# A seven-product form for the first channel product of the last three batches and the tail

## The chip, the cores and the metric

The kernel runs on one core of a Trainium2 chip. The metric is the device time in microseconds of one execution, the median over runs. A profiled execution gives a span, from the first to the last instruction, which is a few microseconds shorter than the device time.

## The reference

Two stages. The first is a linear attention with random features: q and k are projected onto 128 features, put through an exponential, and the output is `q_p @ (k_p.T @ v)` over `q_p @ sum(k_p)`. Its result, per batch 576 tokens by 512, goes into an MLP mixer:

```python
xt = x.transpose(0, 2, 1)
h  = np.maximum(xt @ w_tok1, 0.0) @ w_tok2      # token product, 576 -> 256 -> 576
u  = x + h.transpose(0, 2, 1)
h2 = np.maximum(u @ w_ch1, 0.0) @ w_ch2         # channel product, 512 -> 1536 -> 512
return u + h2
```

There are 8 batches. The change concerns `u @ w_ch1`, the first channel product, and the relu behind it.

## The kernel before

Tokens 0 to 511 of a batch are worked as one block of 512 columns; the 64 last tokens of all eight batches are put together into a ninth block, called the tail (c = 8 in the code, `c == B`). All matmul operands are f16, PSUM sums are f32.

**Order.** Nothing is scheduled by the compiler. Each step is a job with an engine, made by `add`; the jobs are numbered as they are made, and the list `ORDER` at the head of the file gives the order in which they are issued, for all engines at once. So each engine has a fixed queue, and works it in order. `SLOT` gives the ring slot (PSUM bank, SBUF buffer) that each job takes, and `MOVED` the jobs that run on another engine than usual. The stages of neighbouring batches are interleaved: while TensorE does the channel products of batch c, it also does the attention of batch c+1 and the token product.

**A batch on the engines.** Attention (`attention`): TensorE projects (jobs `kp`, `qp`, `kt`, `qt`), ScalarE takes the exponential out of PSUM, VectorE takes a maximum per key (`km`: a reduction over 1,024 elements and a reciprocal; one for each pair of heads, four in a batch), GpSimd scales v with it (`vs_`), TensorE sums over keys (`kv`), and its result, copied to SBUF, is multiplied with q (`num`); VectorE divides (`num_out`). Token product (`token_mix`): `t1_tail`, `t1`, relu, `t2`, then VectorE adds x (`uadd`, four in a batch) and a DMA on SyncE's queue transposes u into uT. Every second batch adds the tails of two batches (`token_tail`).

**First channel product** (`channel_mix`, L967): for each of the 12 blocks of 128 channels, four matmuls of 512 columns over the four blocks of d go into one bank, and one relu (ScalarE, or VectorE where the lists say so) writes r3 in f16. That is 48 matmuls of 512 columns, each with a weight load, for each of the batches and the tail.

**Second channel product** (`channel_out_fast`, L917, L906): from batch 1 on it is done with seven half-size products in place of eight (Strassen's method in Winograd's form). VectorE makes four sums of r3 for each of two parts of 768 elements (the job `go` with g and k, the helper `tt` at L295). Each product is 12 matmuls of 256 columns; the partial results are summed in three banks X, Y and Z, and VectorE reads a bank after each step (`read`, L906). Four sums of the weights are made once (L448).

**Rings.** qT, kT and v (the loaded inputs), x and r1 have three slots each; there are eight PSUM banks.

Of the kernel before, what the change touches and what calls it, by code (L numbers as in the profile page):

```python
# [9 lines left out]
FP32 = mybir.dt.float32  # L10
# [12 lines left out]
    4, 3, 0, 2, 5, 7, 1, 6, 16, 14, 10, 15, 9, 8, 12, 38, 11, -1, -2, -3, -4, -5, -6, -7, -8, 39, 41, 13, 44,  # L23
    42, 21, 40, 47, 45, 48, 76, 22, 46, 77, 67, 43, 68, -4, -6, 120, 18, 105, 78, 107, 82, -3, 49, 71, 106, 122,
    -5, 90, 51, 111, 91, -4, -4, 52, 17, 70, 19, 121, 50, 53, 83, 54, 92, 126, -5, -5, -5, -1, -1, -6, -3, -1,
    72, 69, 30, 108, 79, 110, 84, 112, 80, 96, 55, 81, 127, 113, 74, 73, 123, 109, 75, 28, 128, 124, 85, 114,
    86, 57, 56, 97, 115, 88, 129, 87, 125, -8, 61, 20, 93, 89, 98, 94, 23, 116, 130, 134, 95, 131, 31, 99, 117,
    132, 135, 219, 118, 103, 133, 119, 136, 104, 62, 100, 146, 101, 63, 220, 142, 221, 137, 58, 196, 143, 64,
    102, 24, 59, 144, 25, 147, 60, 66, 138, 460, 145, 205, 139, 65, 197, 222, 225, 140, 223, 206, 29, 148, 199,
    141, 224, 33, 247, 198, 149, 207, 233, 326, 250, 200, 235, 160, 251, 249, 211, 208, 32, 162, 234, 248, 201,  # L30
    156, 210, 253, 161, 158, 157, 163, 330, 174, 209, 254, 202, 236, 170, 238, 226, 237, 172, 204, 27, 159, 227,
    26, 166, 252, 325, 203, 255, 212, 171, 150, 256, 173, 239, 153, 167, 331, 257, 213, 151, 214, 154, 240, 258,
    259, 164, 155, 260, 152, 327, 217, 228, 215, 175, 241, 165, 332, 168, 242, 243, 245, 229, 244, 231, 181,
    169, 176, 246, 216, 182, 232, 177, 230, 218, 183, 261, 186, 262, 329, 264, 263, 328, 178, 265, 184, 266,
    179, 34, 272, 268, 273, 187, 269, 270, 267, 188, 271, 275, 274, 189, 333, 383, 276, 334, 355, 191, 335, 356,
    385, 180, 192, 336, 384, 185, 357, 369, 389, 386, 337, 370, 372, 193, 388, 459, 373, 35, 277, 374, 390, 194,
    36, 293, 371, 461, 387, 278, 465, 358, 294, 341, 361, 338, 295, 359, 360, 285, 343, 375, 362, 340, 344, 342,
    291, 464, 346, 286, 339, 376, 391, 37, 363, 462, 297, 364, 345, 296, 365, 377, 366, 289, 298, 392, 347, 378,
    367, 463, 393, 290, 381, 281, 368, 395, 348, 379, 282, 287, 394, 466, 380, 349, 195, 283, 396, 350, 597,
    382, 351, 353, 595, 284, 299, 354, 292, 190, 352, 279, 288, 300, 478, 397, 280, 472, 400, 473, 305, 306,  # L40
    398, 401, 301, 480, 302, 309, 479, 399, 474, 307, 492, 310, 503, 494, 489, 408, 303, 505, 402, 493, 409,
    406, 504, 403, 313, 490, 407, 491, 404, 314, 467, 506, 308, 517, 316, 304, 519, 405, 468, 469, 518, 410,
    315, 317, 508, 509, 520, 475, 311, 476, 598, 318, 510, 521, 470, 507, 321, 596, 523, 319, 471, 419, 320,
    524, 495, 413, 420, 600, 522, 511, 477, 525, 312, 433, 496, 512, 599, 526, 411, 434, 601, 481, 421, 412,
    414, 513, 323, 527, 497, 528, 425, 482, 498, 514, 529, 429, 729, 426, 602, 501, 530, 515, 431, 516, 734,
    499, 483, 735, 500, 417, 731, 322, 415, 730, 484, 502, 485, 423, 416, 432, 430, 486, 487, 422, 427, 488,
    418, 628, 424, 428, 608, 531, 610, 532, 435, 609, 436, 534, 439, 630, 440, 533, 443, 441, 535, 442, 629,
    437, 538, 444, 542, 642, 539, 653, 540, 438, 654, 536, 644, 541, 447, 324, 543, 655, 537, 643, 625, 448,
    656, 544, 639, 658, 545, 659, 640, 450, 626, 627, 546, 733, 641, 445, 657, 451, 611, 645, 614, 603, 455,
    605, 732, 616, 604, 631, 612, 646, 449, 615, 613, 606, 555, 632, 551, 607, 556, 617, 563, 647, 564, 633,  # L50
    552, 559, 648, 618, 456, 557, 560, 634, 1004, 446, 547, 867, 660, 567, 548, 866, 635, 661, 568, 649, 565,
    662, 558, 452, 665, 458, 736, 651, 561, 666, 652, 865, 553, 650, 619, 562, 637, 549, 620, 554, 638, 621,
    636, 623, 550, 663, 569, 664, 453, 624, 570, 622, 745, 571, 773, 746, 667, 572, 670, 566, 573, 747, 575,
    668, 775, 576, 774, 454, 579, 669, 577, 457, 671, 578, 869, 737, 748, 574, 739, 759, 672, 750, 580, 749,
    676, 673, 678, 738, 761, 677, 674, 760, 583, 740, 675, 585, 679, 584, 680, 787, 765, 762, 776, 586, 778,
    763, 764, 868, 766, 581, 587, 777, 788, 779, 741, 789, 790, 873, 591, 871, 875, 791, 588, 1001, 792, 582,
    1006, 767, 874, 742, 751, 923, 743, 695, 780, 589, 592, 696, 870, 925, 752, 924, 685, 590, 594, 999, 744,
    876, 693, 872, 753, 768, 694, 793, 781, 1000, 689, 686, 754, 782, 771, 699, 772, 794, 757, 755, 769, 758,
# [1013 lines left out]
```

## Time and profile before

| | |
|---|---|
| device time, median of 3 runs | 284.88 us |
| the runs | 284.88, 283.5, 285.11 us |
| span of the profiled execution | 281.1 us |
| TensorE busy | 270.3 us (96%) |
| VectorE busy | 222.4 us (79%) |
| ScalarE busy | 138.6 us (49%) |
| GpSimd busy | 92.0 us (33%) |

The device time of the profiled execution itself is not listed; the three runs lie 2.4 to 4.0 us above its span. In the profile PE is TensorE's matmul queue, PEld its weight loads, DVE VectorE, ACT ScalarE, POOL GpSimd and SP SyncE. A row of a group gives busy time and mean duration; on all engines an instruction's duration overlaps a little with the next one's start, so what an instruction takes of its queue is read from the starts of two neighbours in the timeline.

### The profile page before, as it was taken

Reading aid. Unit: us, or ns where it says so; the run is one execution under the profiler, and the core shown is the slowest. Engines: PE = TensorE matmul, PEld = TensorE weight load, DVE = VectorE, ACT = ScalarE, POOL = GpSimd, SP = SyncE. Lnnn points to the kernel's source line nnn. Section 1 sums busy time; section 2 is a strip of 40 time slices with the busy share of each in tenths; the row PEclk is TensorE's granted clock in tenths of the full one; section 3 lists DMA queues with packets and bytes.
Section 4 is the critical chain, followed back from the end, with each engine's and each line's share of the span. In section 5 each row is a group of like instructions: output and inputs, shape, how many; then the busy total and the mean of one; then the engine's idle time right before and its main releaser. Section 6 shows DMA issues by size and latency. Waiting matters only on the chain.

```text
span 281.1 us, 6278 instructions
## 1 busy us (share of the span) xinstructions
PE 270.3 (96%) x2526; PEld 167.6 (60%) x2526; DVE 222.4 (79%) x462; ACT 138.6 (49%) x288; POOL 92.0 (33%) x116
## 2 busy tenths in 40 slices
PE   6899999999999999999999999999999999999993
PEld 2547546443657755665667647755676467446782
DVE  2589828499999899996997999977995893565992
ACT  1498994049676418743758445734753510031200
POOL 8574994007510872048008710510033000000001
PEclk9999999999999999999999999999999999999999
DMA  6999999999998999997979993960151304030125
GB/s 161 194 189 161 157 169 213 178 191 202 179 218 184 148 172 186 181 198 104 212 178 185 241 135 101 161 156 2 76 97 59 111 0 96 0 149 2 75 90 135
DMA packets 80524, 39.66 MB, mean 141 GB/s; under 512 B 63984, under 2 KB 76016, under 8 KB 80304
## 3 DMA queue, kind: packets, MB, share of 16 engines
q0 software_dynamic: 31744, 17.74, 44.1%
q1 hardware_dynamic: 46832, 15.77, 29.1%
q10 hardware_dynamic: 1920, 5.77, 5.4%
q8 instruction: 19, 0.31, 0.4%
q14 instruction: 9, 0.07, 0.1%
HBM read 35.95 MB, written 16.52 MB: 187 GB/s over the span
## 4 chain that ended last, share of the span: by engine, by line
PE 89%; DVE 3%; DMA 2%; ACT 2%; issue 0%; SPq 0%; DVEq 0%
PE bank L967 32%; PE bank L917 26%; PE bank L791 5%; PE bank L778 5%; PE bank L1001 4%; PE bank L735 3%; PE bank L657 3%; PE bank L702 3%; DMA wc<-in_k_dram 2%; PE bank L669 2%; ACT kp L515 1%; PE bank L845 1%; PE bank L817 1%; PE bank L737 1%; PE bank L771 1%; DVE T L448 1%
## 5 line engine op out<-in xcount | busy, mean ns | idle before, releaser
L967 PE MATMUL bank<-uT,wc 128*128 128x512 f16 x376 | 89.6, 379 | 0.5 <-DVE r L292 0.4
L290 ACT ACTIVATE r<-bank 128x512 f16<-128x512 f32 (+1 forms) x86 | 47.7, 601 | 82.7 <-PE bank L967 61.5
L295 POOL TENSOR_TENSOR vs<-v,vs 128x512 f16<-128x512 f16 x32 | 34.2, 1072 | 94.4 <-DVE vs L683 51.3
L967 PEld LDWEIGHTS <-wc 128*128 128x128 f16 x424 | 38.8, 98 | 38.8 <-issue 1.6
L917 PEld LDWEIGHTS <-r 128*128 128x128 f16 x384 | 36.8, 98 | 8.2 <-issue 1.1
L515 ACT ACTIVATE kp<-bank 128x512 f16<-128x512 f32 x64 | 36.7, 618 | 8.9 <-PE bank L657 7.1
L515 ACT ACTIVATE qp<-bank 128x512 f16<-128x512 f32 x64 | 36.7, 614 | 8.8 <-PE bank L669 5.8
L681 DVE TENSOR_REDUCE km<-kp 128x8 f16<-128x1024 f16 x32 | 38.7, 1208 | 1.2 <-ACT kp L515 1.1
L292 DVE TENSOR_SCALAR r<-bank 128x512 f16<-128x512 f32 (+1 forms) x40 | 26.3, 670 | 15.7 <-PE bank L967 11.3
L745 DVE TENSOR_TENSOR x<-bank,rc 128x320 f16<-128x320 f32 x62 | 30.5, 492 | 2.1
L917 PEld LDWEIGHTS <-S 128*128 128x128 f16 x288 | 28.1, 98 | 5.8 <-issue 0.3
L906 DVE TENSOR_TENSOR o<-u,bank 128x512 f32<-128x512 f16 x28 | 19.0, 679 | 6.2 <-PE bank L917 5.8
L917 PE MATMUL bank<-T,r 128*128 128x256 f16 x192 | 23.8, 273 | 0.0
L917 PE MATMUL bank<-wc,r 128*128 128x256 f16 x192 | 23.6, 273 | 0.0
L917 PE MATMUL bank<-T,S 128*128 128x256 f16 x192 | 23.4, 273 | 0.0
L946 POOL DMA_DIRECT2D out_dram<-o x2 | 1.3, 645 | 61.2 <-issue 61.2
L906 DVE TENSOR_TENSOR o<-o,bank 128x512 f32<-128x512 f32 (+1 forms) x27 | 16.6, 617 | 2.5 <-PE bank L917 1.8
L735 PEld LDWEIGHTS <-qp 128*128 128x128 f16 x256 | 13.5, 98 | 8.1 <-DVE kvsb L286 0.7
L794 DVE TENSOR_TENSOR u<-x,bank 128x512 f16<-128x512 f16 x28 | 17.6, 680 | 0.0
L735 PE MATMUL bank<-kvsb,qp 128*128 128x65 f16 x256 | 15.0, 193 | 0.5 <-DVE kvsb L286 0.5
L791 PE MATMUL bank<-r,w 128*128 128x512 f16 x56 | 14.1, 381 | 0.0
L744 DVE RECIPROCAL rc<-bank 128x5 f32<-128x5 f32 x62 | 11.4, 184 | 2.9 <-PE bank L737 2.2
(119 smaller groups left out, 379.0 us busy)
## 6 DMA issues: line engine op xcount, KB each, us to landing
out_dram<-o ACTq DMA_DIRECT2D x9, 512.0 KB, 2.7
q<-in_q_dram POOLq DMA_DIRECT2D x6, 576.0 KB, 9.7
wc<-in_moe_w_ch_dram POOLq DMA_DIRECT2D x4, 768.0 KB, 9.0
k<-in_k_dram POOLq DMA_DIRECT2D x6, 512.0 KB, 7.8
v<-in_v_dram POOLq DMA_DIRECT2D x6, 512.0 KB, 9.9
out_dram<-o SPq DMA_DIRECT2D x5, 512.0 KB, 3.9
r<-in_q_dram POOLq DMA_DIRECT2D x4, 288.0 KB, 7.5
v<-in_v_dram POOLq DMA_DIRECT2D x4, 256.0 KB, 8.1
```

Source lines behind the costliest of these rows:

```text
L290: nc.scalar.activation(out=out, in_=in_, func=AF.Relu)
L292: nc.vector.tensor_relu(out=out, in_=in_)
L295: (nc.gpsimd if eng == "POOL" else nc.vector).tensor_tensor(**kw)
L515: nc.scalar.activation(out=out, in_=in_, func=AF.Exp, bias=0.0, scale=1.0)
L681: nc.vector.reduce_max(out=mx, in_=kpv, axis=AX.X)
L735: nc.tensor.matmul(ps[:, k, j * 65 : (j + 1) * 65], st, s[:, i, 0 : D + 1], start=True, stop=True)
L745: nc.vector.tensor_tensor(out=t_x[place("x", b)][:, :, (2 * hp + hs[0]) * D : (2 * hp + hs[0] + n) * D].rearrange("p j (i d) -> p i j d", ...
L791: nc.tensor.matmul(ps, w2_of(tb, j), r1[:, tb, :], start=(tb == 0), stop=(tb == NT - 1))
L794: nc.vector.tensor_tensor(out=t_u[place("u", b)][:, j, :], in0=t_x[place("x", b)][:, j, :], in1=bank(n), op=ALU.add)
L906: nc.vector.tensor_tensor(out=o, in0=a, in1=ps, op=ALU.add)
L917: nc.tensor.matmul(ps[:, j * DH : (j + 1) * DH], a[:, cb, j * P : (j + 1) * P], w[:, cb, :], start=(bank_of(b, j0) not in held and j == j0 ...
L967: nc.tensor.matmul(ps, wc1[:, db, cb * P : (cb + 1) * P], moving(db), start=(db == 0), stop=(db == ND - 1))
```

## The change

For c = 5, 6, 7 and the tail the first channel product is done with seven products too (`channel_in_fast`). W1 (512 by 1,536) is cut into four blocks A, u into four blocks of 256 tokens by 256 of d. For each of three groups p of four channel blocks (two in each half of the channels) there are the products P1 to P7 of four matmuls of 256 columns each: 84 matmuls of 256 columns in place of 48 of 512. Around them:

- Four sums of weights (128 by 1,536 elements each), made once, W1 on VectorE and W2, W4, W3 on GpSimd. W3 is written over a block of `wc1`, and so waits for all first products of batch 4.
- Four sums of u (V1 to V4, 128 by 512) for each c. With c = 5: V1 and V3 on GpSimd, V2 and V4 on VectorE.
- For each p: P1's bank X is copied into bank Y on ScalarE (`ka`), so that P2 adds to it; X is copied out in f32 after P6 and after P7 (`kept`, mostly ScalarE); VectorE adds a kept copy to bank Z twice (`summed`: t22, s10); banks Y and X go out through a relu. The two quarters of r3 that `summed` writes get their relu afterwards, in place, in two parts of 1,024 and 512 elements.
- In the second product of c = 5 to 7 bank X is copied to Y on ScalarE after the first product, which leaves out one read of VectorE; its sums are cut in parts of 1,024 and 512 elements in place of 768 and 768, and many of them move to GpSimd.
- The sums lie in slots of kT, qT, v, x and r1 that are taken once and kept.

The lists: up to about 152 us in the trace of before (the first job behind the parting starts at 152.20 us on TensorE, at 151.60 us on VectorE, in batch 4's first channel product) each engine's queue is as before, except that the 23 warming matmuls of the first microseconds are placed otherwise and many banks have other numbers. Behind it, as the new lists have it:

- TensorE, up to the product `k=2` of batch 4's second channel product: 12 blocks of the first channel product of batch 4, three half-size products (one of batch 3, two of batch 4), the token product of batch 5 with its pair of tails, 6 `kv`, 11 `num`, 3 `kp`, 4 `qp`, 1 `qt`.
- VectorE, up to the last sum that this product needs: six `km` (two of batch 5, four of batch 6), eight `num_out`, six relus, four `uadd` and the pair of tails, one `kt_max`, W1, five sums of 768 elements, three reads, three copies `kv_out`. The first of the sums (g=0, k=0) stands behind all six `km`, the `num_out`, the relus, the four `uadd` and W1.
- GpSimd: W2 and W4 behind W1; then three jobs of batch 6 (`vs_`, its tails' factor, `vs_`), one sum of batch 4, `vs_`, W3, `vs_`, V1 of batch 5, and behind V1 the cast of batch 7's q, whose transposed load the `qp` of batch 7 waits for.
- At the end: behind the last matmul of the tail's first product TensorE has one product of batch 7 (12 matmuls) and the 14 half products of the tail (six matmuls each). The tail's sums are shared out over VectorE (parts of 1,024 and 512) and GpSimd (two of 512, two of 1,024).

```diff
+FAST1 = 5
...
-    def engine(self, usual):
+    def engine(self, usual, *others):
...
+    A11, A21, A12, A22 = [wc1[:, 2 * k : 2 * k + 2, e * NH * P : (e + 1) * NH * P] for k in range(2) for e in range(2)]
+    S3 = A21
+    HOME = {1: "kT", 2: "qT", 4: "v"}
+    OF_V = {0: "kT", 1: "qT", 2: "v"}
...
+    def first_weights(plain):
+        for n, a, b, op in ((1, lambda: A21, lambda: A22, ALU.add), (2, lambda: S_of(1), lambda: A11, ALU.subtract),
+                            (4, lambda: A12, lambda: S_of(2), ALU.subtract), (3, lambda: A11, lambda: A21, ALU.subtract)):
+            e_w = engine("DVE", "POOL")
+            def go_w1(n=n, a=a, b=b, op=op, e_w=e_w):
+                tt(e_w, out=S_of(n), in0=a(), in1=b(), op=op)
+            j_W[n] = add(e_w, 0.95, FAST1 - 0.2, go_w1, deps=[*j_wc1, *([j_W[n // 2]] if n in (2, 4) else [*j_W.values()]), *(plain if n == 3 else [])],
+                         take=[("x", "W"), ("r1", "W")] if n == 3 else [(HOME[n], "W")])
...
+        PARTS = (slice(0, 3), slice(3, 6)) if ready is None else (slice(0, 4), slice(4, NH))
+        if ready is None:
+            ready = {(i, e): [[jr[cb + NH * e] for cb in range(p.start, p.stop)] for p in PARTS] for i in range(2) for e in range(2)}
...
+                (1, lambda: (s_of(1), r3(1, 0), r3(1, 1)), ALU.add, [*ready[1, 0][g], *ready[1, 1][g]], ()),
+                (3, lambda: (r3(1, 0), r3(0, 0), r3(1, 0)), ALU.subtract, ready[0, 0][g], (1,)),
+                (2, lambda: (s_of(2), s_of(1), r3(0, 0)), ALU.subtract, ready[0, 0][g], (1,)),
+                (4, lambda: (s_of(3), r3(0, 1), s_of(2)), ALU.subtract, ready[0, 1][g], (2,)),
...
+                job = add(e_sum, 0.5 if c < FAST1 else (0.61, 0.34)[g], key + KEYS["S"] + 0.1 * g + 0.01 * k, go_s,
+                          deps=[*need, *(prev if c < FAST1 else [sums[x][g] for x in after])], take=[("S", c)])
...
+        seed = c >= FAST1 and not tail
...
-                                             start=(bank_of(b, j0) not in held and j == j0 and cb == 0), stop=False, skip_group_check=True)
+                                             start=(bank_of(b, j0) not in held and j == j0 and cb == 0 and not (seed and k == 1)), stop=False, skip_group_check=True)
...
+                if k == 0 and seed:
+                    e_a = engine("ACT", "DVE")
+                    def go_a(e_a=e_a):
+                        copy(e_a, bank(bank_of("Y", 0)), bank(bank_of("X", 0)))
+                    outs["sA", h] = add(e_a, 0.5, key + KEYS["c2"], go_a, deps=[j], take=[("bank", bank_of("Y", 0))])
...
-                    outs["11", h] = read(k, "Y", 0, 0, False, [j, outs["sA", h]], True, j0, j1)
+                    outs["11", h] = read(k, "Y", 0, 0, seed, [j, outs["sA", h]], True, j0, j1)
...
+    def channel_in_fast(c, key, jt):
...
+        for n, what, op, after in (
+            (1, lambda: (v_of(0), u_of(0, 1), u_of(0, 0)), ALU.subtract, ()),
+            (2, lambda: (v_of(1), u_of(1, 1), v_of(0)), ALU.subtract, (1,)),
+            (4, lambda: (v_of(2), u_of(1, 0), v_of(1)), ALU.subtract, (2,)),
+            (3, lambda: (u_of(0, 1), u_of(1, 1), u_of(0, 1)), ALU.subtract, (1,)),
...
+            sums[n] = add(e_sum, 1.0, key - 0.2, go_u, deps=[*jt, *[sums[x] for x in after], *j_W.values()], take=[("V", c)], give=own)
+        ops = {
+            1: ("X", lambda: A11, lambda: u_of(0, 0), [], True), 2: ("Y", lambda: A12, lambda: u_of(1, 0), [], False),
+            6: ("X", lambda: S_of(2), lambda: v_of(1), [sums[2], j_W[2]], False), 5: ("Z", lambda: S_of(1), lambda: v_of(0), [sums[1], j_W[1]], True),
+            7: ("X", lambda: S3, lambda: u_of(0, 1), [sums[3], j_W[3]], False), 3: ("Z", lambda: S_of(4), lambda: u_of(1, 1), [j_W[4]], False),
+            4: ("X", lambda: A22, lambda: v_of(2), [sums[4]], False),
+        for p in range(NH // 2):
...
+                    for t in range(2):
+                        cb = 2 * p + t
+                        for k in range(2):
+                            nc.tensor.matmul(ps[:, 2 * P * t : 2 * P * t + 2 * P], a_[:, k, cb * P : (cb + 1) * P], m[:, :, k, :],
+                                             start=(begin and t == 0 and k == 0), stop=False, skip_group_check=True)
...
+            p1 = product(1, [])
+            e_a = engine("ACT", "DVE")
+            def go_a(e_a=e_a, bank_of=bank_of):
+                copy(e_a, bank(bank_of("Y")), bank(bank_of("X")))
+            ka = add(e_a, 0.5, at, go_a, deps=[p1], take=[("bank", bank_of("Y"))])
+            p2 = product(2, [ka])
+            p5 = product(5, [])
+            e_y = engine("ACT", "DVE")
+            def go_y(e_y=e_y, rows=rows, seen=seen):
+                relu_to(e_y, rows(0, 0), seen("Y"))
+            raw[0, 0].append(add(e_y, 0.5, at, go_y, deps=[p2], give=[("bank", bank_of("Y"))]))
+            p6 = product(6, [ka])
+            kb = kept("b", [p6])
+            p7 = product(7, [kb])
+            kc = kept("c", [p7])
+            t22 = summed("c", "Z", 1, 1, [kc, p5], False)
+            p3 = product(3, [t22])
+            summed("b", "Z", 1, 0, [kb, p3], True)
+            p4 = product(4, [kc])
...
+        for i, e in ((1, 1), (1, 0)):
+            ready[i, e] = []
+            for g, part in enumerate((slice(0, 4), slice(4, NH))):
+                e_p = engine("DVE", "ACT")
+                def go_n(part=part, i=i, e=e, e_p=e_p):
+                    x = t_r3[place("r3", c)][:, NH * e + part.start : NH * e + part.stop, 2 * P * i : 2 * P * i + 2 * P]
+                    relu_to(e_p, x, x)
+                ready[i, e].append([add(e_p, (0.33, 0.2)[g], key + 0.4, go_n, deps=raw[i, e][2 * g : 2 * g + 2])])
...
+        if c == FAST1:
+            first_weights(plain)
+        if c >= FAST1:
+            channel_out_fast(c, key, [], channel_in_fast(c, key, jt))
+            return
```

More of the change, by code (lines that the diff above doesn't have):

```diff
@@ L104 @@
+"ACT", 1311: "ACT", 1312: "SP",
 }
@@ L128, in __init__ @@
         self.held = {}
+        self.whole = [False] * places["bank"]
     def add(self, eng, cost, key, fn, deps=(), take=(), give=(), rows=False, wire=0.0):
@@ L145, in run @@
                 self.warm(-1 - n)
+                self.whole[-1 - n] = True
                 continue
@@ L153, in run @@
                     owner[tag, i] = (tag, name)
+                    if tag == "bank":
+                        assert self.whole[i] or not seeded(name)
+                        self.whole[i] = covered(name)
             j.fn()
@@ L889, in channel_out_fast @@
             ("Z", lambda: s_of(3), W22, sums[4]),
-            ("X", lambda: r3(1, 1), T4, sums[1]),
+            ("X", lambda: r3(1, 1), T4, [*sums[1], *sum(ready[1, 1], [])]),
         )
@@ L982, in channel_mix @@
             j1.heavy = True
+            plain.append(j1)
             e_relu = engine("ACT" if c >= NPE or BY[("r0", "r1")[c]][cb] == "A" else "DVE")
```

140 lines of the change are left out of this document (103 added, 37 removed), and 106 rows, old and new, of the table ORDER.

## The prediction

> **What bounds the kernel now.** I read the page's first part, then busy time by stretches, then TensorE's own waits from 152 us on, then the chain of waits.
>
> ```profile
> span 281.1 us, 6278 instructions
> PE 270.3 (96%) x2526; PEld 167.6 (60%) x2526; DVE 222.4 (79%) x462; ACT 138.6 (49%) x288; POOL 92.0 (33%) x116
> 152.20:180.00 27.80, 27.80 (x259) 17.31 (x256) 25.25 (x54) 15.57 (x31) 10.22 (x12) 1.00 0.97 168
> 180.00:208.00 28.00, 28.00 (x266) 17.93 (x265) 24.07 (x50) 16.14 (x34) 4.22 (x4) 1.00 0.43 92
> 236.00:266.00 30.00, 30.00 (x190) 18.41 (x188) 18.82 (x33) 4.93 (x11) 0.00 (x0) 1.00 0.12 47
> PE bank L771 <- DVE x L745: 0.3, 1, 0.3
> 161.85 4.32 PE bank L967 x20
> 173.10 0.55 PE bank L845 x4
> 265.73 10.52 PE bank L917 x96
> 276.27 0.42 DVE o L906
> ```
>
> In the rows of stretches the second number is TensorE's busy time, then weight loads, VectorE, ScalarE, GpSimd. TensorE is busy throughout, with the granted clock at 1.00, and has one wait of 0.3 us behind 152 us. So its work is the time: less of it is a gain to the last tenth, and every new wait is a loss that nothing later gives back. VectorE is second: 25.25 of 27.80 us at 152, 18.82 of 30.00 at the end.
>
> **What TensorE saves.** 20 matmuls of 512 columns took 4.32 us in the chain, 0.216 each; 96 of 256 columns, each with its own weight load, took 10.52, 0.1096 each. Before: 48 x 0.216 = 10.37 us for a first channel product; after: 84 x 0.1096 = 9.21. Four of them save 4 x 1.16 = 4.65 us. That is the whole gain.
>
> **Stretch A: VectorE's queue in front of batch 4's second channel product.** The lists part at 152.20 us (TensorE) and 151.60 (VectorE). I add up both queues to the product k=2 of batch 4, with what a job takes of its queue, from the starts of neighbours.
>
> ```profile
> 156.11 0.41 PE L702 MATMUL bank<-vs,kp 128*128 128x65 f16 x8
> ...
> 156.41 0.40 PE L702 MATMUL bank<-vs,kp 128*128 128x65 f16 x8
> ...
> 158.59 0.28 PE L735 MATMUL bank<-kvsb,qp 128*128 128x65 f16 x4
> ...
> 158.74 0.28 PE L735 MATMUL bank<-kvsb,qp 128*128 128x65 f16 x4
> ...
> 166.09 0.39 PE L669 MATMUL bank<-qT,omT 64*128 64x512 f16 x2
> 166.32 0.38 PE L771 MATMUL bank<-x,w1t 64*128 64x512 f16 x2
> 166.54 0.39 PE L657 MATMUL bank<-omT,kT 64*128 64x128 f16 x8
> 166.86 1.90 PE L778 MATMUL bank<-x,w1m 128*128 128x512 f16 x8
> ```
>
> TensorE: 12 channel blocks of four matmuls (48 x 0.216 = 10.4), three half-size products (36 x 0.1096 = 3.9), token product of batch 5 (16 x 0.216 = 3.5, and 0.22 for its tail rows), its pair of tails 0.55, six kv at 0.30, eleven num at 0.15, three kp at 0.32, four qp at 0.23, one qt at half of that: 24.0 us, so TensorE could begin the product at 176.2.
>
> ```profile
> 60.65 1.37 DVE L851 TENSOR_TENSOR ut<-x,bank 64x512 f16<-64x512 f16 x2
> 62.05 0.69 DVE L591 TENSOR_REDUCE kmt<-kpt 128x4 f16<-128x512 f16 x1
> ...
> 63.08 1.21 DVE L681 TENSOR_REDUCE km<-kp 128x8 f16<-128x1024 f16 x1
> ...
> 64.51 0.91 DVE L448 TENSOR_TENSOR T<-wc,T 128x1536 f16<-128x1536 f16 x1
> 65.33 1.81 DVE L448 TENSOR_TENSOR T<-wc 128x1536 f16<-128x1536 f16 x1
> 160.80 0.29 DVE L286 CAST kvsb<-bank 128x130 f16<-128x130 f32 x1
> 161.00 0.19 DVE L744 RECIPROCAL rc<-bank 128x5 f32<-128x5 f32 x1
> ...
> 162.44 0.18 DVE L744 RECIPROCAL rc<-bank 128x5 f32<-128x5 f32 x1
> ...
> 163.06 1.28 DVE L292 TENSOR_SCALAR r<-bank 128x512 f16<-128x512 f32 x2
> 164.26 0.18 DVE L744 RECIPROCAL rc<-bank 128x5 f32<-128x5 f32 x1
> ...
> 168.41 0.55 DVE L295 TENSOR_TENSOR r<-r 128x768 f16<-128x768 f16 x1
> 168.88 0.55 DVE L295 TENSOR_TENSOR S<-S,r 128x768 f16<-128x768 f16 x1
> ...
> 170.41 0.68 DVE L906 TENSOR_TENSOR o<-u,bank 128x512 f32<-128x512 f16 x1
> 171.01 1.28 DVE L794 TENSOR_TENSOR u<-x,bank 128x512 f16<-128x512 f16 x2
> ```
>
> VectorE, each from one start to the next: km 1.43 (63.08 to 64.51), kt_max 1.03 (62.05 to 63.08), pair of tails 1.40, W1 0.82 (the 1,536 elements of 64.51), kv_out 0.20, num_out 0.62, relu 0.60 (two in 1.20), a sum of 768 elements 0.47, a read 0.60, a uadd also 0.60 (same shape). Six km 8.6, eight num_out 5.0, six relus 3.6, four uadd 2.4, the pair 1.4, kt_max 1.0, W1 0.8, five sums 2.35, three reads 1.8, three kv_out 0.6: 27.6 us. From 151.60 that ends at 179.2, and the product needs the last sum. So TensorE stands 3.0 us here, even if VectorE never waits. Two thirds of it is there at batch 5's token product already, whose x comes from the last num_out. The old list had none of batch 6's four km and no W1 ahead of these sums.
>
> The other price is the two engines on the same data path.
>
> ```profile
> 64.85 1.48 POOL L295 TENSOR_TENSOR vs<-v,vs 128x512 f16<-128x512 f16 x1
> 66.28 0.58 POOL L364 DMA_DIRECT2D k<-in_k_dram  x1
> L295 POOL TENSOR_TENSOR vs<-v,vs 128x512 f16<-128x512 f16 x32 | 34.2, 1072 | 94.4 <-DVE vs L683 51.3 <-PE bank L669 22.2 <-PE bank L917 13.8
> L295 POOL TENSOR_TENSOR T<-vt,T 128x1024 f16<-128x1024 f16 x1 | 1.9, 1937 | 0.0
> uT<-u SPq DMA_TRANSPOSE x7, 4.8
> q<-in_q_dram POOLq DMA_DIRECT2D x6, 576.0 KB, 9.7
> qT<-q SPq DMA_TRANSPOSE x6, 5.9
> ```
>
> At 64.85 GpSimd's vs_ and VectorE's weight sums met: vs_ took 1.48 in place of 1.07, and the second sum 1.81 where the one before took 0.91; it ended 0.86 us after vs_ did (65.33 + 1.81 = 67.14 against 66.28). They took turns. The Trainium skill, page "SBUF — State Buffer", section "Who interferes with whom", has this as a rule: a VectorE instruction with two SBUF inputs and a GpSimd instruction that reads SBUF exclude each other for a whole instruction. It speaks against this change, and this row agrees; by it stretch A comes to 4.3 or 5.1 us below, without it to 3.0.
>
> Here W3 takes 1.5 x 1.94 = 2.9 us on GpSimd. It starts when batch 4's last channel block is done, at 152.2 + 18.9 (TensorE's jobs up to there) + 2 (already lost) = 173.1, and ends about 176.1. VectorE reaches its first sum of r3 at 151.6 + 23.3 (its jobs up to there) = 174.9, and waits until 176.1: 1.2 us more. V1 of batch 5 waits for uT (last uadd 174.7, a transpose 4.8, so 179.6), and may hold up the last sum by 0.8 us more. So stretch A costs 3.0 (VectorE's queue alone), 4.3 (with W3) or 5.1 us (with V1). I take 4.3.
>
> **Stretch B: batches 5 to 7.** Behind A VectorE gets, for each batch, six adds at about 0.60, two to four relus in place and some sums, less the seed's read and the sums that GpSimd takes: about +3.5 us a batch, against 2.6 to 3.9 us idle in 28 in the rows above, and 4.3 us that TensorE now trails. ScalarE has 15 copies and relus for 12; it was at 16.14 of 28. GpSimd's long sums (1.07 for 512, 1.94 for 1,024) fill its queue, but TensorE's delay covers them. Batch 7's q is cast behind V1: about 180.7 + 9.7 + 5.9 = 196.3 us, while the first qp of batch 7 comes 15.7 us of TensorE's jobs behind the start of A's product (four half-size products 5.3, 18 of the new ones 7.9, t1 0.9, small ones 1.6), which is at 176.2 + 4.3: 196.2. So 0 to 1.5 us in B; I take 0.5.
>
> **Stretch C: the end.** Behind the last matmul of the tail's first product (time 0) TensorE has 12 + 5 x 6 matmuls of work, 4.6 us, before it needs the two S2 sums. VectorE: an add 0.8 (0.68 and some 0.1 for the start), in-place relu (not in the trace; 0.2 to 0.6 by the rows of a 768-element sum and of a relu, I take 0.35), sums of 512 and 1,024 elements (0.31 and 0.63, by 0.47 for 768): 2.1 us. Then GpSimd's S2 part, 1.07, to 3.2; VectorE's own part behind it to 3.8, or behind GpSimd's next sum of 1.94, to 5.8. That is no wait, or 1.2 us. Then S3: GpSimd to 5.7, VectorE's part behind it to 6.1, or behind another 1.07 to 7.1, and a read of 0.42 (276.27), against TensorE at 5.9: 0.6 to 1.6 us. C costs 0.6 to 2.8; I take 1.7. Behind TensorE's end all is as before, a read and the stores.
>
> **Sum.** -4.65 + 4.3 + 0.5 + 1.7 = +1.85 us: a span of 282.95 for 281.1. The median of the runs is 284.88, 3.8 above this span; I add the change to it: **286.7 us**.
>
> **The rivals.**
> - The gain survives. Place: stretch A. Price: only VectorE's queue, 3.0 us, with W3 done before the sums come up; B and the end lose nothing, as their sums fall in the good order. -4.65 + 3.0 = -1.65, 283.2 us. For it: TensorE's 4.65 us are certain, and stretch B has room. It decides at a total of 3.2 us of waits. Chance 0.30.
> - It evens out: A at 3.6 (the middle of its first two bounds), B at 0.2, the end at 0.9: 284.9 us. Chance 0.22.
> - Taking turns spreads: from 176 us to the end some 30 sums of VectorE meet GpSimd's, and the delays no longer fit into TensorE's lag: A 5.1, B 1.5, C 2.8 is +4.75, 289.6 us. For it: GpSimd goes from 4.22 busy us in 28 to over half. Against it: in B TensorE's own delay leaves time. Chance 0.15.
>
> The forecast has 0.33. Could the change not do what it says, with 256-column matmuls waiting for weights? The 96 of the chain, one weight load each, went at 0.1096, so no.
>
> **The numbers.** A difference of 0.5%, 1.4 us, is about what a measurement of this kernel tells from none. Faster by more: 0.30. Within it: 0.22. Slower: 0.33 + 0.15 = 0.48. The range must hold the gain case down to waits of 2.5 us (282.7) and the spread case up to 290.0; the slower cases alone reach from 286.3 to 290.0.
>
> **What would show it.** TensorE's work falls by about 4.6 us: the plain first product is left in batches 0 to 4, and 336 matmuls of 256 columns stand for the rest. In the waits of TensorE stands a wait for VectorE at batch 4's L917 product, about 4 us with the one before batch 5's token product; the first sums of batch 4 last over 0.55 us while GpSimd is in W3. The last 15 us show one or two waits of TensorE for S2 or S3. Wrong would be: TensorE without waits near 176 us (then the gain survives), or waits mainly between 200 and 260 us, or a last part longer than 3 us over before.

## The result, and the profile after

The changed kernel takes **294.49 us** (median of four runs), the kernel before 284.19 in the runs beside it: ratio 1.036, 95% interval 1.028 to 1.043. A second set, on another occasion, gave 296.19 against 284.46, ratio 1.042 (1.036 to 1.049). So it is some 10 us slower; 286.7 was forecast, with 290.0 as the upper end. Medians, here and in the table below, are of all runs, while ratios leave out slow executions, over 1.5% above the fastest of their kernel (here one of 301.96 us, in `mend_w_split` two of four, in `gps_write` the profiled one). The profiled execution took 296.1 us, its span is 294.0.

First the page of the changed kernel: the span, the busy times, TensorE and its granted clock in 40 slices of 7.35 us, and the shares of the chain that ended last. Its line numbers are those of the changed file: L971 is the second channel product (L917 before), L1126 the plain first product (L967), L1059 the new one, L312 a sum (L295), L960 a read (L906), L1072 an add of the new product, L793 the division of the attention, L309 a relu.

```profile
span 294.0 us, 6656 instructions
PE 272.0 (93%) x2670; PEld 183.4 (62%) x2670; DVE 240.2 (82%) x468; ACT 156.2 (53%) x321; POOL 147.8 (50%) x148
PE   6899999999986999999999998799898998999983
PEclk9999999999999999999999999599999999999999
PE 55%; DVE 22%; DMA 10%; issue 4%; POOL 3%; ACT 3%; SPq 0%; DVEq 0%; POOLq 0%; ACTq 0%
```

Where TensorE was busy without a break, it now has gaps: one in the 12th and 13th slice (about 88 us, ahead of every new sum), and several from the 25th on. One slice has half the clock. VectorE holds 22% of the chain that ends last, where it held 3% in the kernel before:

```profile
PE 89%; DVE 3%; DMA 2%; ACT 2%; issue 0%; SPq 0%; DVEq 0%
```

The stretches (columns as in the prediction: length, TensorE, weight loads, VectorE, ScalarE, GpSimd, clock):

```profile
152.20:180.00 27.80, 27.67 (x275) 16.83 (x274) 26.07 (x51) 21.16 (x45) 24.93 (x21) 1.00 1.06 155
180.00:208.00 28.00, 24.42 (x248) 18.98 (x245) 23.50 (x42) 13.66 (x29) 12.69 (x9) 0.88 0.41 99
208.00:236.00 28.00, 25.77 (x266) 19.60 (x265) 26.24 (x49) 15.88 (x32) 14.01 (x12) 1.00 0.15 39
...
184.50:191.40 6.90, 4.99 (x34) 3.79 (x35) 5.38 (x12) 0.81 (x3) 4.66 (x4) 0.51 0.58 113
```

In the stretch from 180 us TensorE stands 3.6 us, and behind the gap it runs 6.9 us at a clock of 0.51: the 4.99 us that it is busy there cost about 2.5 us more than at full clock (an estimate: half of it). No term of the prediction had that. The Trainium skill, page "TensorE: Matmul & The Clock Gate", section "What's actually happening", has windows of 3.4 us whose activity sets the clock to half or full. The traces of all these kernels agree: every stretch of half clock that the span's end doesn't cut lasted 3.4 or 6.8 us.

TensorE's waits behind 157 us, where the lists part in this trace, and VectorE's batch 4 sums at the worst place, with GpSimd's instructions of the same time:

```profile
PE bank L971 <- DVE o L960: 2.7, 3, 1.7
PE bank L971 <- DVE S L312: 1.9, 1, 1.9
PE bank L750 <- DVE x L793: 1.3, 1, 1.3
PE bank L1059 <- DVE qT L312: 0.8, 1, 0.8
PE bank L705 <- DVE r L1072: 0.6, 1, 0.6
...
179.86 2.04 DVE L312 TENSOR_TENSOR r<-r 128x768 f16<-128x768 f16 x1
181.82 1.41 DVE L312 TENSOR_TENSOR S<-S,r 128x768 f16<-128x768 f16 x1
183.26 0.69 DVE L960 TENSOR_TENSOR o<-u,bank 128x512 f32<-128x512 f16 x1
183.87 0.79 DVE L312 TENSOR_TENSOR r<-r 128x768 f16<-128x768 f16 x1
184.58 1.77 DVE L312 TENSOR_TENSOR S<-S,r 128x768 f16<-128x768 f16 x1
...
178.07 3.42 POOL L312 TENSOR_TENSOR wc<-wc 128x1536 f16<-128x1536 f16 x1
181.45 1.37 POOL L312 TENSOR_TENSOR vs<-v,vs 128x512 f16<-128x512 f16 x1
182.78 1.46 POOL L312 TENSOR_TENSOR kT<-uT 128x512 f16<-128x512 f16 x1
...
184.77 1.16 POOL L312 TENSOR_TENSOR uT<-uT 128x512 f16<-128x512 f16 x1
```

A sum of 768 elements takes 0.55 us when alone (168.41 in the trace before). Here it takes 2.04, 1.41, 0.79 and 1.77. The first ends at 181.90, just behind GpSimd's weight sum (178.07 + 3.42 = 181.49); the last at 186.35, just behind the sum of 184.77 + 1.16 = 185.93. The read in between has one operand in PSUM and keeps its 0.69.

Below, **excess** is what VectorE's instructions behind 155 us took above the shortest of their line and shape in the whole trace, added up over those that took at least 0.15 us more: 14.2 us here, 0.0 in the kernel before. **Idle** is TensorE's idle time behind 155 us, gaps of over 0.15 us: 8.1 us here, 0.25 before. Three of the other waits have the same picture. Rows of VectorE, and GpSimd's that meet them:

```profile
206.93 1.79 DVE L642 TENSOR_TENSOR vbd<-rct,mask 128x8 f16<-128x8 f16 x1
...
221.03 1.96 DVE L312 TENSOR_TENSOR v<-uT,qT 128x512 f16<-128x512 f16 x1
...
238.23 1.90 DVE L309 TENSOR_SCALAR r<-r 128x512 f16<-128x512 f16 x1
...
206.54 2.13 POOL L312 TENSOR_TENSOR S<-S,r 128x1024 f16<-128x1024 f16 x1
...
220.59 2.12 POOL L312 TENSOR_TENSOR S<-r,S 128x1024 f16<-128x1024 f16 x1
...
237.86 2.12 POOL L312 TENSOR_TENSOR S<-r 128x1024 f16<-128x1024 f16 x1 [13.86 <-DVE r L309]
```

Even an instruction of eight elements a row stands 1.6 us, and behind each of these rows TensorE has one of its waits (208.7, 222.4 and 240.5 us).

The gap at 88 us is another matter. A view of waits and the list of the transfers issued from 78 to 80 us show it:

```profile
DVE o L960 <- DMA out_dram<-o: 4.2, 1, 4.2
out_dram<-o SPq DMA_DIRECT2D x1, 256.0 KB, 10.3
out_dram<-o ACTq DMA_DIRECT2D x1, 256.0 KB, 10.3
```

The new list gives batch 1's first read the o slot from which batch 0's last store still reads; the old list gave it the other slot. That store, on ScalarE's queue, lands 10.3 us after its issue, and so does one of the same size that SP issues 0.2 us ahead of it; two others, issued at 63.5 and 64.1 us, took 2.7 and 2.9. So it isn't the queue; what made the two late stays open. (They took 9.3 and 10.0 us in the kernel before, where nobody waited for them.) Matched product by product, TensorE is 1.4 us late at 85 us and 5.0 at 90, with not one new sum made.

### The profile page after: what moved, and what is told of

It is laid out like the page before. It is cut to its first block, busy times and chain, and to the rows that moved or that the text cites. A ratio compares the mean times of both kernels' runs of the same rounds, so it can differ in the third digit from the quotient of the medians.

```text
span 294.0 us, 6656 instructions
## 1 busy us (share of the span) xinstructions
PE 272.0 (93%) x2670; PEld 183.4 (62%) x2670; DVE 240.2 (82%) x468; ACT 156.2 (53%) x321; POOL 147.8 (50%) x148
## 4 chain that ended last, share of the span: by engine, by line
PE 55%; DVE 22%; DMA 10%; issue 4%; POOL 3%; ACT 3%; SPq 0%; DVEq 0%; POOLq 0%; ACTq 0%
PE bank L971 15%; PE bank L1126 12%; PE bank L1059 7%; DMA wc<-in_moe_w_ch_dram 4%; DVE o L960 4%; PE bank L1161 4%; DMA out_dram<-o 4%; DVE S L312 3%; PE bank L826 3%; PE bank L839 3%; DMA wc<-in_k_dram 2%; DVE r L309 2%; DVE r L1072 2%; DVE x L793 2%; PE bank L750 2%
## 5 line engine op out<-in xcount | busy, mean ns | idle before, releaser
L312 POOL TENSOR_TENSOR vs<-v,vs 128x512 f16<-128x512 f16 x32 | 34.6, 1088 | 62.1 <-DVE vs L731 55.5
L307 ACT ACTIVATE r<-bank 128x512 f16<-128x512 f32 (+1 forms) x75 | 42.5, 603 | 34.7 <-PE bank L1126 20.6
L1126 PE MATMUL bank<-uT,wc 128*128 128x512 f16 x232 | 56.3, 379 | 0.1
L971 PEld LDWEIGHTS <-r 128*128 128x128 f16 x384 | 36.8, 98 | 9.1 <-issue 3.3
L971 PEld LDWEIGHTS <-S 128*128 128x128 f16 x288 | 28.2, 99 | 12.3 <-DVE S L312 7.2
L1126 PEld LDWEIGHTS <-wc 128*128 128x128 f16 x232 | 20.7, 97 | 20.4 <-issue 1.3
L793 DVE TENSOR_TENSOR x<-bank,rc 128x320 f16<-128x320 f32 x62 | 30.5, 491 | 2.1
L971 PE MATMUL bank<-T,S 128*128 128x256 f16 x192 | 24.4, 279 | 7.1 <-DVE S L312 5.4
L960 DVE TENSOR_TENSOR o<-u,bank 128x512 f32<-128x512 f16 x28 | 19.0, 679 | 7.3 <-DMA out_dram<-o 4.2
L971 PE MATMUL bank<-T,r 128*128 128x256 f16 x192 | 23.9, 275 | 1.0 <-DVE o L960 1.0
L971 PE MATMUL bank<-wc,r 128*128 128x256 f16 x192 | 23.5, 273 | 0.3 <-DVE r L1072 0.3
L309 DVE TENSOR_SCALAR r<-bank 128x512 f16<-128x512 f32 (+1 forms) x27 | 17.7, 660 | 6.8 <-PE bank L826 4.0
L1059 PEld LDWEIGHTS <-wc 128*128 128x128 f16 x192 | 18.5, 100 | 2.9
L783 PEld LDWEIGHTS <-qp 128*128 128x128 f16 x256 | 14.4, 99 | 6.1 <-issue 0.2
L312 POOL TENSOR_TENSOR r<-r 128x1024 f16<-128x1024 f16 (+1 forms) x6 | 10.6, 1774 | 14.8 <-PE bank L826 14.8
L312 POOL TENSOR_TENSOR S<-r 128x512 f16<-128x512 f16 (+2 forms) x5 | 7.2, 1444 | 19.0 <-DVE r L309 14.2
L960 DVE TENSOR_TENSOR o<-o,bank 128x512 f32<-128x512 f32 (+1 forms) x24 | 14.3, 607 | 2.8 <-PE bank L971 2.8
L1059 PE MATMUL bank<-uT,wc 128*128 128x256 f16 x108 | 15.9, 284 | 0.0
```

Of the source, the lines that this page charges most:

```text
L307: nc.scalar.activation(out=out, in_=in_, func=AF.Relu)
L309: nc.vector.tensor_relu(out=out, in_=in_)
L312: (nc.gpsimd if eng == "POOL" else nc.vector).tensor_tensor(**kw)
L783: nc.tensor.matmul(ps[:, k, j * 65 : (j + 1) * 65], st, s[:, i, 0 : D + 1], start=True, stop=True)
L793: nc.vector.tensor_tensor(out=t_x[place("x", b)][:, :, (2 * hp + hs[0]) * D : (2 * hp + hs[0] + n) * D].rearrange("p j (i d) -> p i j d", ...
L960: nc.vector.tensor_tensor(out=o, in0=a, in1=ps, op=ALU.add)
```

## The experiments

The first question was what the 10 us are: the **turns** (VectorE's sums stand while GpSimd's sums read), VectorE's **queue** (it has too much to do), the **length** of GpSimd's sums, or the **slot**. In the table, ratio is to the kernel before in the same runs.

| run | us | ratio (95%) | idle | excess |
|---|---|---|---|---|
| before | 284.2 | | 0.25 | 0.0 |
| changed | 294.5 | 1.036 (1.028 to 1.043) | 8.1 | 14.2 |
| changed, again | 296.2 | 1.042 (1.036 to 1.049) | 7.7 | 13.8 |
| o_swap | 293.7 | 1.035 (1.030 to 1.039) | 7.9 | 14.7 |
| before_o_late | 285.3 | 1.003 (1.000 to 1.007) | 0.25 | 0.0 |
| w3_dve | 298.2 | 1.050 (1.046 to 1.055) | 8.1 | 12.9 |
| gps_write | 294.6 | 1.037 (1.032 to 1.042) | 9.2 | 2.2 |
| gps_short | 291.4 | 1.024 (1.018 to 1.029) | 4.3 | 1.2 |
| sums_dve | 295.7 | 1.041 (1.035 to 1.047) | 8.8 | 1.7 |
| sums_dve_act | 297.5 | 1.048 (1.042 to 1.054) | 9.8 | 1.7 |
| split | 293.6 | 1.035 (1.028 to 1.042) | 8.6 | 10.0 |
| gps_short_o | 283.1 | 0.996 (0.994 to 0.999) | 1.6 | 1.7 |
| mend_w | 293.5 | 1.029 (1.023 to 1.035) | 6.8 | 13.5 |
| mend_w_split | 292.7 | 1.017 (1.010 to 1.025) | 6.2 | 7.3 |
| mend_o | 294.3 | 1.039 (1.033 to 1.045) | 9.2 | 15.5 |
| gps_half_o | 288.9 | 1.019 (1.014 to 1.023) | 5.5 | 8.1 |
| gps_two_o | 282.8 | 0.996 (0.993 to 0.999) | 1.9 | 3.4 |
| gps_wait_o | 283.1 | 0.996 (0.993 to 1.000) | 1.2 | 2.1 |

**1. The slot alone, in both kernels.** The edit is in the list of ring places: every 0 and 1 that o gets from batch 1 on exchanged.

> The changed kernel with the two ring slots of o exchanged from batch 1 on, nothing else. Slot theory: 3.6 us of the loss come before any new sum: VectorE stood 4.16 us for the store of batch 0 that still held the slot which the list gives to batch 1's first read. With the other slot that wait is gone, everything behind starts about 3.6 us earlier, time 289 to 290.5 for the 292.9 of the changed kernel. Sums theory alone (all of the loss lies behind 157 us, the early stall is caught up later): within 1 us of 292.9.

> The kernel before with the two ring slots of o exchanged from batch 1 on. Slot theory: batch 1's first read now waits for the same store, 3 to 4.2 us, TensorE's queue has nothing to fill it, and the kernel before goes to 287 to 288.5 from 284.2. Rival (the store's landing time was an accident of one execution, or the lists absorb it): within 1 us of 284.2.

The changed kernel's early wait goes (no gap of TensorE near 88 us in the trace), but the time is 293.7. In the kernel before, the wait appears (VectorE stands 1.9 us, the store landed in 7.4) and the time rises by 0.3%, with an interval that touches zero. Both forecasts of the slot theory, 289 to 290.5 and 287 to 288.5, were wrong: the slot's wait is real in the trace, but its worth in time was below what these runs can tell. The wait isn't in every trace of a kernel with that list either: in `sums_dve` below the store landed in 6.5 us and nobody waited.

**2. One weight sum moved to VectorE, and the same kernel again.**

```
 MOVED:  - 820: "POOL"   + 820: "DVE"      (W3)
```

> The changed kernel with one weight sum, W3, moved from GpSimd (3.42 us) to VectorE (about 0.9). Turns theory (VectorE's sums wait for GpSimd's sums, a whole instruction at a time): the sums of batch 4 that took 0.99, 2.04, 1.41 and 1.77 us fall to 0.55 to 1.1, TensorE's wait of 3.6 us at 182 falls to 1 to 2 us, the half clock behind it goes, 2 to 4.5 us faster. Queue theory (VectorE simply has too much to do there): its queue grows by 0.9, so 0 to 0.9 us slower.

> The changed kernel as it is, once more, as the yardstick of the three runs beside it. All theories: 292.9 to 296, with waits of TensorE near 87 us (3.5) and 182 us (3.6 in two parts).

At 1.050 it is no better than the yardstick's 1.042; the gain of 2 to 4.5 us that the turns theory forecast did not come. The weight sum itself and the sums behind it:

```profile
180.56 1.56 DVE L313 TENSOR_TENSOR wc<-wc 128x1536 f16<-128x1536 f16 x1
182.04 1.41 DVE L313 TENSOR_TENSOR S<-r 128x768 f16<-128x768 f16 x1
...
185.25 1.51 DVE L313 TENSOR_TENSOR S<-S,r 128x768 f16<-128x768 f16 x1
187.40 1.06 DVE L313 TENSOR_TENSOR r<-r 128x768 f16<-128x768 f16 x1
```

GpSimd brought its next instructions forward into the free place and met the same sums; the gaps there add up to 3.64 us where they were 3.58. So it isn't this one sum alone.

**3. GpSimd's sums as writes.** These kernels leave GpSimd's new sums out and write zeros in their place, so their output is not the reference's. In `go_w1`, `go_s` and `go_u` (shortened):

```
 if eng == "POOL":
+    for _ in range(3):            # gps_short: one write
+        nc.gpsimd.memset(out, 0.0)
```

> The changed kernel in which each sum that GpSimd makes (first operands, second operands, weights) is replaced by three writes of zeros into the same place, which read nothing; the numbers are not the reference's. GpSimd's per-head products of v stay. Turns theory: VectorE's excess of 14.2 us behind 157 us falls under 3, TensorE's idle time there from 8.3 to under 2.5 us, the clock stays full: 7 to 10 us faster, 283 to 286. Queue theory: VectorE's durations fall but TensorE goes on waiting for its queue, over 290. Part of a gain could also come from GpSimd being done earlier, since its writes wait for fewer operands.

> As with the three writes of zeros, but one write for each of GpSimd's sums, some 0.35 to 1.0 us where the sums take 1.15 to 2.1; the numbers are not the reference's. In the run with three writes VectorE was free of GpSimd (excess 1.2 us) and TensorE still stood 9.2 us behind 157 us, but then for GpSimd, whose writes took 1.37 times as long as its sums. GpSimd theory (its long sums cost twice: by turns with VectorE, and by their own length): with both gone TensorE's idle time behind 157 us falls under 3 us and the clock stays full, 283 to 286. VectorE's queue alone: idle time stays at 6 us or more, over 290.

With three writes the excess falls from 14 to 2.2 us and nothing is gained. That looked like the end of the turns theory. But three writes of 1,024 elements take 2.97 us, 1.4 times a sum, and TensorE now waited 8.1 us for GpSimd itself. The sizes were badly chosen. With one write the time falls to 291.4. Both are short of the 283 to 286 that the theories with GpSimd in them forecast, and what is left in the second is almost all stores:

```profile
DVE o L966 <- DMA out_dram<-o: 8.5, 2, 4.3
```

The second of these is new in sight. Batch 3's second store has its data at 160 us; in the old list ScalarE issues it, in the new one it stands in SP's queue behind the transposes of batch 5's u and of the tails, is issued at 183.5 in this run, lands 8.5 us later, and batch 4's read needs that slot.

**4. All sums on VectorE.** 33 jobs (`go_s`, `go_u`, `go_w1`) moved from POOL to DVE; in the second run 26 copies and relus from DVE to ACT as well.

> The changed kernel with all 33 sums of GpSimd (4 kinds: first operands, second operands, weights, batch 4's) on VectorE, same places in the list. VectorE gets some 17 us of sums in the last 135 us and loses the 14 us that it stood for GpSimd's. GpSimd theory: the chains get shorter (0.4 to 0.7 us for 1.15 to 2.1), idle time of TensorE 3 to 5 us, 3 to 6 us faster than the changed kernel. VectorE's queue alone: about 3 us slower.

> As the one with all sums on VectorE, and 26 copies and relus of VectorE (about 10 us) on ScalarE, which was at half load. GpSimd theory: idle time of TensorE under 3 us, 5 to 8 us faster than the changed kernel. VectorE's queue alone: better than the one with the sums alone by 3 us or more, but near the changed kernel.

No excess to speak of (1.7 us), no gap of 3.6 us, and still 295.7 and 297.5: in the first, idle time comes back in seventeen pieces of 0.2 to 1.4 us. Its stretches:

```profile
152.20:180.00 27.80, 25.58 (x246) 14.74 (x245) 26.81 (x51) 18.64 (x40) 16.32 (x19) 1.00 0.96 145
180.00:208.00 28.00, 26.05 (x283) 19.99 (x281) 25.13 (x57) 17.55 (x36) 1.35 (x1) 1.00 0.49 98
208.00:236.00 28.00, 26.05 (x266) 19.88 (x264) 25.98 (x53) 12.81 (x26) 4.28 (x4) 1.00 0.20 49
```

VectorE is at 25 to 27 us of 28: it has hardly any room for the sums. Both forecasts of the GpSimd theory (3 to 6 and 5 to 8 us faster) missed. Moving work to ScalarE, in an order made for other engines, brought nothing; why stays open.

**5. Both stores mended, GpSimd's sums as one write.** `ORDER`: job 594, the store, directly behind 593; o's places exchanged as in 1.

> The run with one write of zeros for each GpSimd sum (the numbers are not the reference's), and two moves that cost no engine anything: o's ring slots exchanged from batch 1 on, and the second store of batch 3, whose data is there at 160 us, issued at 162 in place of 183 (in the run before VectorE stood 4.3 and 4.2 us for these two stores, and TensorE 3.66 and 3.59, with 3.4 us of half clock behind each). Slot theory: both idle times and the half clocks go: 291.4 less 7.2 less up to 3.4 is 281 to 284, below the kernel before (284.5): with GpSimd out of the way and the slots right the 4.95 us of TensorE's work come through. If other waits come up in their place: over 287.

283.1: below the kernel before, 8.3 us less than the same kernel with the two store waits. The second store's wait is hidden in the changed kernel: there the store is issued at 182.4 us too, and VectorE waits for no store behind 155 us; it shows once the sums are quicker. For the first store traces and times don't agree: without its wait the spans of `o_swap` and `mend_o` are 2.9 and 3.1 us shorter than the changed kernel's, so in the traces it is not hidden, while the medians differ by only 0.2 to 2.5 us. How much of the 8.3 us belongs to which store stays open.

**6. Sums in pieces, and weight sums elsewhere.** In `split` GpSimd makes each sum in pieces of 256 elements (768 for the weights); in `mend_w` the stores are mended, W1 and W2 come behind batch 3's residual adds, W4 behind batch 6's q cast, and W3 on VectorE behind batch 4's sums.

> The changed kernel with GpSimd's sums in pieces: same engine, same data, but 256 elements an instruction (768 for the weights). By 1.15 us for 512 and 2.12 for 1,024 a piece should take 0.67, all of GpSimd's sums some 20% more. Turns theory (a whole instruction at a time): VectorE's longest waits fall from 1.5 to under 0.7 each, its excess behind 157 us from 14 to 6 to 9 us, and TensorE's idle time from 8.3 to 4 to 6 us: 2 to 4 us faster than the changed kernel (294.5 to 296.2 in its own runs). GpSimd's length theory: its queue gets longer, so 1 to 3 us slower.

> The changed kernel with all sums real, the same two moves for o, and the weight sums out of the crowded place: W1 and W2 some 45 us earlier, W4 30 us earlier (GpSimd idle there), W3 on VectorE behind batch 4's sums. Turns theory: batch 4's sums run at 0.55 to 1.0, the wait of 3.6 us at 182 goes under 1 us with the half clock behind it, the early one too; what is left is 4.6 us of idle time behind 205 us: 286 to 289. If VectorE's queue is the bound at batch 4: the wait at 182 stays over 2 us, 290 or more.

> The same with GpSimd's sums in pieces of 256 elements. Turns theory: idle time behind 205 us falls from 4.6 to 2 to 3 us as well, 284 to 287, even with the kernel before. GpSimd's length theory: slower than the one with whole sums by 1 to 2 us.

Pieces alone, at 1.035 beside the changed kernel's 1.036 and 1.042, are not told from none; 2 to 4 us were forecast. The excess falls to 10.0 us, and 3.8 of them are in one place, the first of these pairs of VectorE's and GpSimd's rows:

```profile
189.56 4.21 DVE L316 TENSOR_TENSOR qT<-uT,kT 128x512 f16<-128x512 f16 x1
...
189.70 3.79 POOL L319 TENSOR_TENSOR S<-r,S 128x256 f16<-128x256 f16 x6
...
265.20 0.61 DVE L316 TENSOR_TENSOR S<-S,r 128x512 f16<-128x512 f16 x1
265.74 0.89 DVE L316 TENSOR_TENSOR v<-uTt,qT 128x512 f16<-128x512 f16 x1
266.55 0.89 DVE L316 TENSOR_TENSOR S<-r,S 128x512 f16<-128x512 f16 x1
...
264.23 2.92 POOL L319 TENSOR_TENSOR S<-r,S 128x256 f16<-128x256 f16 x4 [2.34 <-PE bank L1066]
```

In the first, VectorE did not get in between six pieces issued one behind the other: its sum of 0.42 us ended at 193.77, behind the last of them, and TensorE stood 3.3 us. In the second, three such sums ran in among the pieces at 0.61 to 0.89 us each, and most rows of this trace are of that kind. What decides it the runs don't show.

The two with the weight sums moved missed their forecasts as well (286 to 289, and 284 to 287 with pieces). In `mend_w` GpSimd has no weight sum near batch 4's sums, and its wait is still 1.93 us long: these sums now meet GpSimd's V1 and V3 and its products of v. With pieces, 1.017 is the best of the versions that compute everything; all are slower than the kernel before.

**7. Reads or length: a table of two by two.** All four have the stores mended. `mend_o` has the real sums, `gps_two_o` two writes for each, `gps_half_o` the sums of operands over half their width (the weight sums and batch 5's sums of u stay whole). Only `mend_o` computes the reference's output.

> The changed kernel with all sums as they were, o's slots exchanged and batch 3's second store issued early: full length, with reads. Both theories: the early idle time of 3.5 us is gone, TensorE's idle time behind 155 us stays at 8 to 8.5 us: 290.5 to 293.5.

> The mended kernel in which GpSimd's sums of second operands (and of first operands behind batch 5) are made over half their width: 0.67 for 1.15 and 1.15 for 2.12 us, with reads (the numbers are not the reference's; weight sums stay whole). Turns theory: VectorE still meets nearly as many of them, the excess falls only with the length, from 14 to 7 to 9 us, idle time 4 to 6: 286.5 to 290. Length theory: as fast as one write, 283 to 286.

> As the run with one write for each sum and mended stores, but two writes: no reads, 1.93 us for 2.12 and 1.05 for 1.15 (the numbers are not the reference's). Turns theory: VectorE's excess stays under 2 us and the time near that of one write: 283 to 286. Length theory: TensorE stands 5 us or more for GpSimd's results, 288 to 291.

| | full length | about half |
|---|---|---|
| GpSimd's sums read SBUF | 294.3 (mend_o) | 288.9 (gps_half_o) |
| only writes | 282.8 (gps_two_o) | 283.1 (gps_short_o) |

Without reads the length makes no difference; with reads it is worth 5.4 us, and the reads themselves 11.5 us at full length. One thing was left: a write needs no operands, so GpSimd might simply run ahead. The last run has a sum of 8 columns a block ahead of the two writes, which waits for all the operands:

> As the run with two writes, with a sum of 8 columns of each block ahead of them, which waits for the same operands as the whole sum and reads SBUF for some 0.2 us (the numbers are not the reference's). GpSimd is then as long as with real sums or longer, and waits for the same results. Turns theory: VectorE's excess stays under 4 us, 283 to 286. If it was the waiting for operands that the writes saved: TensorE's idle time behind 155 us goes to 6 us or more, 289 to 293.

283.1. GpSimd's compute behind 155 us is 69.7 us here and 69.8 in `mend_o`, so it is as busy and waits for the same results; only the long reads are gone. The pages, first of `mend_o`, then of `gps_wait_o`:

```profile
PE 270.6 (93%) x2670; PEld 182.8 (63%) x2670; DVE 241.4 (83%) x468; ACT 156.3 (54%) x321; POOL 147.7 (51%) x148
```

```profile
PE 268.6 (96%) x2670; PEld 181.7 (65%) x2670; DVE 228.5 (81%) x468; ACT 156.0 (55%) x321; POOL 147.3 (52%) x214
```

And batch 4's sums, first in `mend_o`, then in `gps_wait_o` with the product that needs them:

```profile
176.75 3.05 DVE L319 TENSOR_TENSOR r<-r 128x768 f16<-128x768 f16 x1
179.72 1.41 DVE L319 TENSOR_TENSOR S<-S,r 128x768 f16<-128x768 f16 x1
...
182.47 1.77 DVE L319 TENSOR_TENSOR S<-S,r 128x768 f16<-128x768 f16 x1
```

```profile
176.24 0.56 DVE L328 TENSOR_TENSOR r<-r 128x768 f16<-128x768 f16 x1
...
178.37 0.55 DVE L328 TENSOR_TENSOR S<-S,r 128x768 f16<-128x768 f16 x1
...
178.99 1.48 PE L987 MATMUL bank<-T,S 128*128 128x256 f16 x12
```

So the turns are shown: same engine, same busy time, same operands waited for, and 11 us less when the reads are short. The zeros are no rival: TensorE's matmuls on kT's slot, which GpSimd fills for batch 5, are 0.109 us apart in both.

## Why the prediction was right and wrong

- **TensorE's saving, 4.65 us: the price of a matmul right, the saving not whole.** In the changed kernel's chain 40 of the new matmuls in a row took 4.39 us, 0.1098 each, as 0.1096 was forecast from the 96. But from the same point of the lists on, TensorE is busy 126.98 us in the kernel before and 123.95 in `gps_wait_o`, the second number of these rows: 3.0 us less, and 3.2 and 2.9 in `gps_short_o` and `gps_two_o`.

```profile
197.99 4.39 PE bank L1059 x40
...
149.00:276.30 127.30, 126.98 (x1077) 82.48 (x1074) 101.56 (x207) 48.53 (x97) 22.75 (x26) 1.00 0.45 95
...
150.92:276.60 125.68, 123.95 (x1221) 96.45 (x1218) 107.76 (x213) 65.82 (x130) 77.97 (x124) 1.00 0.44 97
```

  By shape, the matmuls of 256 columns took 0.6 us more than 0.1096 each would give, and the small ones of the attention 0.9 more than before.

- **"Lists kept up to batch 4": a term that wasn't there.** The prediction charged nothing ahead of 152 us, because the engines' queues are the same. The ring places are not, and that brought 3.6 us of waiting for a store. The 1.4 us ahead of it are no more than executions differ by: the kernel before with o's places exchanged, too, is 1.2 late at 82 us. Worth in time: not told from zero while the sums are late, 8.3 us for both stores once they aren't (runs 3 and 5).
- **Stretch A, 4.3 us: the place right, the two prices wrong both ways.** "VectorE's queue 3.0 us" is nothing: without the long reads its last sum ends at 178.92 and the product starts at 178.99, with no gap of TensorE from 155 to 205 us. The error is countable, and it stands in the account of the new lists too: six relus and three kv_out were charged to VectorE, and ahead of the last sum the trace has two relus on it (169.40 and 171.35 us) and no kv_out; ScalarE makes the others. That is 2.4 and 0.6 us, all of the 3.0. "W3 1.2, V1 0.8" was far too little: the turns made all of the 3.58 us. W3 came when it was forecast (178.07, less the 5.1 that this trace is late, for 173.1), VectorE's first sum 2.5 us earlier (177.54 less 5.1, for 174.9), and so W3 fell into the middle of the sums. I charged one meeting each; every one of batch 4's five sums met one, with vs_ as well as with the new sums.
- **The half clock, about 2.5 us: not in the sum.** Two gaps of 1.66 and 1.92 us, 0.5 us apart, were enough; in `mend_w` one of 1.93 was followed by 3.4 us of half clock.
- **Stretch B, 0.5 us (0 to 1.5): wrong.** 3.3 us in five gaps between 208 and 246 us, from the rows at 206.93, 221.03, 238.23 and their like. "TensorE's own delay leaves time" failed: VectorE, busy 26.24 of 28 us from 208 on, has no slack to use it, since it loses time in the same turns. With the reads short B has two gaps, 0.54 and 0.68.
- **Stretch C, 1.7 us (0.6 to 2.8): right, at the low end.** Behind the tail's first product (it ends at 278.0) there is no wait for S2 and one of 0.78 us for S3, of 0.6 to 1.6 forecast. GpSimd's sum ends 6.0 us behind it, VectorE's part at 6.3 and the read at 6.7, while TensorE is free at 5.9; 5.7, 6.1 and 5.9 were forecast. Two gaps of 0.44 us together lie ahead of it, at 268 and 270 us.
- **The sum.** The spans are 12.9 us apart. In the profile 5.1 of it come ahead of the sums; then TensorE is idle 8.0 us more and busy 0.1 us more (the half clock's 2.5, less some 2.4 that its work saves here), and the end behind its last matmul is 0.3 shorter.
- **The rivals.** "Taking turns spreads" (0.15) had the mechanism; its 4.75 us was still too small, since it added one or two meetings to each stretch instead of counting the excess over all of VectorE's sums. "The gain survives" holds only with the reads out of the way, and then 1.1 to 1.4 us of the 4.65 came through, 0.4%, with intervals that end at 0.9986 to 0.9997. The rest: 1.4 to 1.7 us of work not saved and 1 to 1.7 us more idle time (0.25 us before); these traces are also 1.0 to 1.9 us late where the lists part, about as much as executions differ by.

The row that carried the warning was in the prediction: 1.81 us for 0.91 at 65.33. The Trainium skill, page "SBUF — State Buffer", section "Who interferes with whom", limits it to GpSimd instructions that read, and lets writes go free beside a sum of two SBUF inputs. Runs 3 and 7 agree: 14.2 and 15.5 us of excess with reads, 1.2 to 3.4 without. The rule was known; counting how often it would strike was the step left out.

## What to carry to other kernels

When work goes to an engine because it is idle, count the meetings, not the load: here GpSimd's compute behind 155 us, 71 us where it was 12, cost VectorE 14 us, and the reads in it cost the kernel 11 us (run 7), more than twice the gain that was hoped for. Before charging a queue difference of a few us, see whether it is larger than the error of the two sums it comes from, and look in the lists for the engine of each job that is charged. A list that is "the same" is the same only if its ring places and the engines of its stores are too; and a wait that costs nothing now may be the bound once the one ahead of it is mended.

## What was not expected of the hardware

- Pieces don't always give VectorE a turn: one sum took 4.21 us behind six back-to-back GpSimd instructions of 0.63 each, three others 0.61 to 0.89 in among such pieces.
- In-place relus with a single SBUF input stand too: 1.90 us at 238.23, where one of twice the width took 0.42 just before. The same section of the Trainium skill has contention for such instructions too, in the modes that use both ports.
- A store of 256 KB took 2.7 us when issued at 63.5 us and 10.3 when issued at 78.6, and then on SP's queue and on ScalarE's alike; a median over three stores hid it.
- TensorE was at half clock after gaps of under 2 us each, and in `mend_w` after a single one of 1.93.
